# Sixty-four-column pairs for a recurrent attention kernel's large matmuls, and a new split of its DMA queues

## The chip, the cores and the metric

The kernel runs on one core of a Trainium2 chip, in one launch. The metric is the device time of that launch in microseconds, lower is better. TensorE is called PE below, VectorE DVE, ScalarE ACT, GpSimd POOL and SyncE SP.

## What is computed

Four layers are run over one sequence of 2048 tokens of width 512: attention with a recurrent memory (A), a dense layer (B), A again, B again, each with a layer norm in front and a residual around it. A and B use the same weights both times.

```python
def A(x, mem):                         # x: 2048 x 512, mem: 8 x 512
    for s in range(64):                # segments of 32 tokens
        h = concat(mem, x[32*s : 32*s+32])              # 40 x 512
        q, k, v = h @ Wq, h @ Wk, h @ Wv                # 32 heads of 128
        p = softmax(mask(q @ k.T * 128**-0.5))          # per head 40 x 40
        o = concat_heads(p @ v) @ Wo                    # 40 x 512
        mem = o[:8]                                     # goes into the next segment
        out[32*s : 32*s+32] = o[8:]
B = lambda x: relu(x @ w1) @ w2                         # 512 -> 1376 -> 512
x = x + A(layernorm(x), mem0);  x = x + B(layernorm(x))
x = x + A(layernorm(x), mem0);  x = x + B(layernorm(x))
```

The memory ties each segment to the one before it, so the 64 segments of a layer come strictly in turn.

## The kernel before, in words

The two A layers run interleaved: the second starts four segments (`DELTA = 4`) after the first. Step k of 68 handles segment k of the first layer (stream 0) and segment k-4 of the second (stream 1). Steps 0 to 3 have stream 0 alone (40 columns), steps 4 to 63 both (80 columns), steps 64 to 67 stream 1 alone. Weights lie in SBUF throughout.

A step is made of these pieces; the lines are those that the profile shows:

- `step_values`: V for the step's tokens, from the transposed activations `HT`. Steps 4 to 63 use `values` (L973), pairs of matmuls with 64 output columns side by side in the array. Step 0 uses `values_direct` (L1038), steps 1 to 3 use `values_narrow` (L992), four matmuls of 32 columns side by side, whose results reach `V0` by DMA (`place_values`, L1026).
- `queries_keys` (L1074): Q and K of four heads per PSUM bank, 256 matmuls of 128 output columns by 80 a step, evicted to SBUF by ACT or DVE (`copy_on`, L894 and L896).
- `scores` (L1103, 40 columns, pairs side by side), the softmax on DVE and ACT, the transpose of P by a matmul with the identity (`across`, L646), and `attend` (L1187, P times V).
- `project` (L1214): the sum over all heads times `Wo`, 128 matmuls of 128 columns by 80, into one PSUM bank. DVE copies its memory columns into the next step's `HT` (L1230), and this starts the next step's Q and K.
- every second step `finish_pair`: residual, layer norm, dense layer (`across`, L646) for 64 tokens of each layer.

The half of V that doesn't depend on the memory (the first 16 rows of each segment of layer 1) is computed ahead in groups of 128 tokens: groups 0 to 5 (`EARLY = 5`) during start-up (`early_values`, L973), the rest in pairs of groups in later steps (`late_values`, L944, whole 128-column matmuls), spread as work that can fill waits. They go to DRAM (`vh`) and come back by DMA, a segment at a time. Normalized rows go to DRAM too (`xh`) and are read back by `load_group`.

The order of all instructions on all engines is fixed when the program is built, by a list scheduler in the kernel's text (`Plan.order`). It goes by a table of priorities per operation (`PLACE` for PE, `AHEAD` for the others), some constants (`RULE`, `PERIOD`), and costs. Each PE operation has a column mode: `WHOLE` (128 columns), `COL64` (pairs of 64), or `EITHER`, which takes the mode in which the array happens to be; the plan counts `TURN` for each change of mode. `across` writes an `EITHER` operation out: with 64 columns, each 128-column matmul becomes two, on two halves of the array. Before the change the scores and `values` are `COL64`; transposes, `attend` and the first dense matmuls `EITHER`; Q, K, projection and `late_values` `WHOLE`.

DMA queues before: the first quarter of Wv from SP, the other weights from POOL in the order Wv, Wq and Wk by halves, Wo by halves; x rows of the early groups from ACT; early V stores (`vh`) from POOL behind the weights; early `xh` stores from SP, held back until step 1's V is placed. Everything later is on SP.

Of the kernel before, what the change touches and what calls it, by code (L numbers as in the profile page):

```python
# [26 lines left out]
WHOLE, COL64, EITHER, COL32 = range(4)  # L27
TURN = 0.096

RULE = (0.0731, 331.4491, 505.4188, 866559925356557.625)  # L30
PERIOD = 46.2777
PLACE = {
    ("attend.mmu0.0", 0): -152.667, ("attend.mmu0.0", 1): -118.912, ("attend.mmu0.0", 2): -639.225,
    ("attend.mmu0.0", 3): 328.193, ("attend.mmu0.0", 4): -173.499, ("attend.mmu0.0", 5): 386.967,
    ("attend.mmu0.0", 6): 449.133, ("attend.mmu1.0", 0): -183.38, ("attend.mmu1.0", 1): 433.744,
    ("attend.mmu1.0", 2): 361.711, ("attend.mmu1.0", 3): 441.403, ("attend.mmu1.0", 4): -122.568,
    ("attend.mmu1.0", 5): 199.077, ("attend.mmu1.0", 6): 581.404, ("attend.mmu2.0", 0): -862.741,
    ("attend.mmu2.0", 1): -762.821, ("attend.mmu2.0", 2): -99.412, ("attend.mmu2.0", 3): -218.396,
    ("attend.mmu2.0", 4): -720.778, ("attend.mmu2.0", 5): -60.014, ("attend.mmu2.0", 6): -142.579,
    ("attend.mmu3.0", 0): -166.299, ("attend.mmu3.0", 1): -129.893, ("attend.mmu3.0", 2): -1226.967,  # L40
    ("attend.mmu3.0", 3): 67.821, ("attend.mmu3.0", 4): -136.693, ("attend.mmu3.0", 5): -20.817,
    ("attend.mmu3.0", 6): 293.466, ("attend.mmu4.0", 0): 65.898, ("attend.mmu4.0", 1): -215.881,
    ("attend.mmu4.0", 2): 381.601, ("attend.mmu4.0", 3): 412.604, ("attend.mmu4.0", 4): -130.21,
    ("attend.mmu4.0", 5): -853.627, ("attend.mmu4.0", 6): 948.075, ("dense_layer.mm.0", 1): 732.94,
    ("dense_layer.mm.0", 3): 740.199, ("dense_layer.mm.0", 6): 839.326, ("dense_layer.mm.1", 1): -969.556,
    ("dense_layer.mm.1", 3): -286.677, ("dense_layer.mm.1", 6): 67.604, ("dense_layer.mm.2", 1): 398.19,
    ("dense_layer.mm.2", 3): 243.499, ("dense_layer.mm.2", 6): 419.477, ("dense_layer.mm.3", 1): 627.889,
    ("dense_layer.mm.3", 3): 181.496, ("dense_layer.mm.3", 6): 643.035, ("dense_layer.mm.4", 1): 161.37,
    ("dense_layer.mm.4", 3): 390.622, ("dense_layer.mm.4", 6): 400.054, ("dense_layer.mm.5", 1): 594.567,
    ("dense_layer.mm.5", 3): 753.248, ("dense_layer.mm.5", 6): 345.325, ("finish_pair.turn.0", 1): -144.39,  # L50
    ("finish_pair.turn.0", 3): -761.751, ("finish_pair.turn.0", 6): -878.802, ("g0", 2): -907.97,
    ("g1", 2): 259.128, ("g2", 2): -170.342, ("g3", 2): -266.685, ("g4", 2): -99.976, ("g5", 2): 565.774,
    ("late_values.mmv0.0", 0): 283.731, ("late_values.mmv1.0", 0): -248.92, ("late_values.mmv2.0", 0): -1018.714,
    ("late_values.mmv3.0", 0): 469.169, ("late_values.mmv4.0", 0): -1001.105, ("late_values.mmv5.0", 0): 1.489,
    ("late_values.mmv6.0", 0): -868.467, ("late_values.mmv7.0", 0): 433.155, ("layernorm.turn.0", 1): 337.759,
    ("layernorm.turn.0", 3): 441.922, ("layernorm.turn.0", 6): -292.588, ("layernorm.turn.1", 1): -863.663,
    ("layernorm.turn.1", 3): -167.818, ("layernorm.turnr.0", 0): -153.966, ("layernorm.turnr.0", 4): 426.349,
    ("layernorm.turnr.1", 0): 374.651, ("layernorm.turnr.1", 4): 594.017, ("prepare.turns.0", 2): -916.093,
    ("project.mm.0", 0): 352.884, ("project.mm.0", 1): 403.52, ("project.mm.0", 2): 426.265,
    ("project.mm.0", 3): 475.549, ("project.mm.0", 4): -8.363, ("project.mm.0", 5): 481.308,  # L60
    ("project.mm.0", 6): 364.213, ("project.mm.1", 0): 360.97, ("project.mm.1", 1): 250.905,
    ("project.mm.1", 2): 395.025, ("project.mm.1", 3): 90.611, ("project.mm.1", 4): -154.497,
    ("project.mm.1", 5): 342.487, ("project.mm.1", 6): -140.762, ("project.mm.2", 0): 69.475,
    ("project.mm.2", 1): 427.61, ("project.mm.2", 2): -910.526, ("project.mm.2", 3): 539.171,
    ("project.mm.2", 4): -962.774, ("project.mm.2", 5): 327.765, ("project.mm.2", 6): 570.292,
    ("project.mm.3", 0): 234.432, ("project.mm.3", 1): 212.581, ("project.mm.3", 2): 219.168,
    ("project.mm.3", 3): 1057.658, ("project.mm.3", 4): 374.948, ("project.mm.3", 5): 458.206,
    ("project.mm.3", 6): 1049.752, ("project.mm.4", 0): -906.842, ("project.mm.4", 1): -226.675,
    ("project.mm.4", 2): -119.077, ("project.mm.4", 3): 366.414, ("project.mm.4", 4): -955.316,
    ("project.mm.4", 5): 408.222, ("project.mm.4", 6): -222.974, ("queries_keys.mmu0.0", 0): -319.479,  # L70
    ("queries_keys.mmu0.0", 1): -311.142, ("queries_keys.mmu0.0", 2): -195.441,
    ("queries_keys.mmu0.0", 3): -783.942, ("queries_keys.mmu0.0", 4): -856.389,
    ("queries_keys.mmu0.0", 5): -1226.512, ("queries_keys.mmu0.0", 6): -189.749,
    ("queries_keys.mmu0.1", 0): -126.555, ("queries_keys.mmu0.1", 1): -875.245,
    ("queries_keys.mmu0.1", 2): -230.758, ("queries_keys.mmu0.1", 3): -218.806, ("queries_keys.mmu0.1", 4): -924.83,
    ("queries_keys.mmu0.1", 5): -998.214, ("queries_keys.mmu0.1", 6): -798.535, ("queries_keys.mmu0.2", 0): 1.933,
    ("queries_keys.mmu0.2", 1): -915.221, ("queries_keys.mmu0.2", 2): -763.206,
    ("queries_keys.mmu0.2", 3): -815.004, ("queries_keys.mmu0.2", 4): -155.478,
    ("queries_keys.mmu0.2", 5): -920.249, ("queries_keys.mmu0.2", 6): -766.935, ("queries_keys.mmu0.3", 0): -285.59,
    ("queries_keys.mmu0.3", 1): -134.747, ("queries_keys.mmu0.3", 2): 7.492, ("queries_keys.mmu0.3", 3): -23.601,  # L80
    ("queries_keys.mmu0.3", 4): -292.473, ("queries_keys.mmu0.3", 5): -193.042,
    ("queries_keys.mmu0.3", 6): -173.541, ("queries_keys.mmu1.0", 0): -40.306,
    ("queries_keys.mmu1.0", 1): -1010.704, ("queries_keys.mmu1.0", 2): -94.937,
    ("queries_keys.mmu1.0", 3): -233.672, ("queries_keys.mmu1.0", 4): -212.713,
    ("queries_keys.mmu1.0", 5): -961.418, ("queries_keys.mmu1.0", 6): -321.925,
    ("queries_keys.mmu1.1", 0): -965.925, ("queries_keys.mmu1.1", 1): -223.66, ("queries_keys.mmu1.1", 2): -323.504,
    ("queries_keys.mmu1.1", 3): 20.112, ("queries_keys.mmu1.1", 4): -146.653, ("queries_keys.mmu1.1", 5): -223.193,
    ("queries_keys.mmu1.1", 6): -158.937, ("queries_keys.mmu1.2", 0): -823.694,
    ("queries_keys.mmu1.2", 1): -932.252, ("queries_keys.mmu1.2", 2): -231.6, ("queries_keys.mmu1.2", 3): -250.634,
    ("queries_keys.mmu1.2", 4): 237.43, ("queries_keys.mmu1.2", 5): -250.953, ("queries_keys.mmu1.2", 6): -993.941,  # L90
    ("queries_keys.mmu1.3", 0): -189.715, ("queries_keys.mmu1.3", 1): -231.672,
    ("queries_keys.mmu1.3", 2): -257.674, ("queries_keys.mmu1.3", 3): -300.812,
    ("queries_keys.mmu1.3", 4): -145.268, ("queries_keys.mmu1.3", 5): -37.546, ("queries_keys.mmu1.3", 6): -183.014,
    ("queries_keys.mmu2.0", 0): 140.663, ("queries_keys.mmu2.0", 1): -210.356, ("queries_keys.mmu2.0", 2): -294.536,
    ("queries_keys.mmu2.0", 3): -112.732, ("queries_keys.mmu2.0", 4): 320.259, ("queries_keys.mmu2.0", 5): 215.543,
    ("queries_keys.mmu2.0", 6): -122.288, ("queries_keys.mmu2.1", 0): 428.309, ("queries_keys.mmu2.1", 1): 92.511,
    ("queries_keys.mmu2.1", 2): -899.997, ("queries_keys.mmu2.1", 3): 229.222, ("queries_keys.mmu2.1", 4): 280.866,
    ("queries_keys.mmu2.1", 5): 161.233, ("queries_keys.mmu2.1", 6): 27.508, ("queries_keys.mmu2.2", 0): 204.746,
# [82 lines left out]
    ("values_direct.ev", 1): -11.513, ("values_narrow.ev", 1): -7.969,  # L181
}

LOAD = {("v", 0): 4.4, ("v", 1): 3.8, "o": 2.95}
REST, SLOW = 2.75, 6.0

EARLY, SPREAD = 5, (0, 0, 2, 4, 4, 6, 8, 8)


def t_mm(n):  # L190
    return max(0.025, 0.0025 + n / 2400)


# [211 lines left out]
def kernel(  # L405
# [387 lines left out]
    def prepare_group(g, gate=(), first=None):  # L793
# [26 lines left out]
        if g <= EARLY:  # L820
            early_values(g, xnT)
# [530 lines left out]
```

## Time and profile before

| | |
|---|---|
| runs, us | 1633.72, 1636.3, 1640.62 (median 1636.3) |
| the profiled execution | 1633.76 us in all, of which the span of the profile is 1632.0 |
| mean TensorE clock granted | 0.997 of full |
| DVE, ACT, POOL busy | 1111.6, 1052.5, 140.1 us (68%, 64%, 9%) |
| longest rows | L1074 Q and K 355.7 + 349.3 us, L1214 344.5 us, L973 265.9 us |
| DMA moved | 63.89 MB, at 369 and 231 GB/s in the first two fortieths of the span, at most 51 after |
| weights from POOL, median issue to landing | Wq 21.3, Wk 25.8, Wo 36.7 us |

How to read it: the profile shows a matmul from its start to a modelled end, some 0.2 us later, while the next one starts 0.036 us after it. So a "busy" PE hides short waits. The distance between starts is what counts. An engine's own idle time is shown in square brackets with the event that ended it.

### The profile page before, as it was taken

What the parts mean: (1) busy time and instruction counts of PE and PEld (TensorE: products, weight loads), DVE (VectorE), ACT (ScalarE), POOL (GpSimd) and SP (SyncE); (2) the same over time, 40 slices, a digit from 0 to 9 for tenths busy, and PEclk for the clock granted to TensorE, in tenths of its full rate; (3) what the DMA queues carried; (4) which work ended last, traced back from release to release, by engine and by line L of the source; (5) the groups of instructions that cost most, each with busy time, mean ns of one, the idle gap of its engine ahead of it and who ended that gap; (6) DMA issues with size and microseconds to landing.
All of it is one profiled execution on the core that took longest, in us unless ns stands there. A gap on an engine that the chain in (4) does not pass through costs nothing.

```text
span 1632.0 us, 88442 instructions
## 1 busy us (share of the span) xinstructions
PE 1589.6 (97%) x39898; PEld 1377.3 (84%) x39992; DVE 1111.6 (68%) x3091; ACT 1052.5 (64%) x2655; POOL 140.1 (9%) x352
## 2 busy tenths in 40 slices
PE   7999999999999999999999999999999999999997
PEld 4788888888888888888888888888888888888886
DVE  4566776776676676677667667667667767766765
ACT  5566666676666666666667666666666666666664
POOL 3100000000000100000100000100000000000000
PEclk9999999999999999999999999999999999999999
DMA  9720101110110110110110111110110100000000
GB/s 369 231 51 21 27 22 27 41 28 22 28 24 22 41 26 22 25 34 19 38 29 22 28 25 28 35 28 20 28 28 22 26 21 22 19 18 18 18 6 6
DMA packets 47097, 63.89 MB, mean 39 GB/s; under 512 B 17784, under 2 KB 33440, under 8 KB 46720
## 3 DMA queue, kind: packets, MB, share of 16 engines
q1 hardware_dynamic: 41136, 39.09, 10.0%
q0 software_dynamic: 4704, 18.35, 2.9%
q8 instruction: 313, 5.13, 1.4%
q10 hardware_dynamic: 880, 0.80, 0.2%
q14 instruction: 64, 0.52, 0.1%
HBM read 33.50 MB, written 11.93 MB: 28 GB/s over the span
## 4 chain that ended last, share of the span: by engine, by line
PE 92%; DMA 3%; DVE 2%; ACT 2%; issue 1%; POOL 0%; ACTq 0%; SPq 0%; POOLq 0%; DVEq 0%
PE work L1074 37%; PE st L1214 18%; PE fill L973 14%; PE fill L646 10%; PE work L1187 4%; PE work L1103 4%; DMA Wo_sb<-in_A_Wo_dram 2%; PE work L646 2%; PE fill L944 2%; ACT OT L894 1%; DVE HT L1230 0%; PE fill L992 0%; DMA vw<-in_A_x_dram 0%; ACT es L1125 0%; ACT PT L1168 0%
## 5 line engine op out<-in xcount | busy, mean ns | idle before, releaser
L1074 PE MATMUL work<-HT,Wk_sb 128*128 128x80 bf16 (+1 forms) x8704 | 355.7, 199 | 9.6 <-DVE HT L1230 8.8
L1074 PE MATMUL work<-HT,Wq_sb 128*128 128x80 bf16 (+1 forms) x8704 | 349.3, 199 | 1.3 <-DVE HT L1230 0.9
L1214 PE MATMUL st<-OT,Wo_sb 128*128 128x80 bf16 (+1 forms) x8704 | 344.5, 199 | 4.5 <-ACT OT L894 2.5
L1214 PEld LDWEIGHTS <-Wo_sb 128*128 128x128 bf16 x8704 | 324.9, 99 | 28.0 <-issue 5.2
L1074 PEld LDWEIGHTS <-Wq_sb 128*128 128x128 bf16 x8704 | 320.4, 99 | 26.4 <-issue 15.1
L1074 PEld LDWEIGHTS <-Wk_sb 128*128 128x128 bf16 x8704 | 321.6, 99 | 16.4 <-DVE HT L1230 13.3
L894 ACT CAST qT<-work 128x320 bf16<-128x320 f32 (+1 forms) x534 | 219.5, 412 | 76.8 <-PE work L1074 32.4
L973 PE MATMUL fill<-Wv_sb,HT 128*64 128x512 bf16 x2048 | 265.9, 381 | 0.0
L894 ACT CAST kT<-work 128x320 bf16<-128x320 f32 (+1 forms) x510 | 209.9, 412 | 82.5 <-PE work L1074 49.1
L894 ACT CAST OT<-work 128x320 bf16<-128x320 f32 (+1 forms) x404 | 158.1, 417 | 119.8 <-PE work L1187 117.3
L1168 ACT ACTIVATE PT<-work,half 128x320 bf16<-128x320 f32 (+2 forms) x384 | 170.9, 468 | 67.1 <-PE work L646 47.0
L894 ACT CAST vw<-fill 128x512 bf16<-128x512 f32 x203 | 119.0, 586 | 92.5 <-PE fill L973 82.0
L1114 DVE TENSOR_TENSOR es<-work,maskb 128x320 f32<-128x320 f32 (+2 forms) x340 | 136.8, 404 | 45.2 <-PE work L1103 40.3
L1170 DVE TENSOR_SCALAR PT<-work,half 128x160 bf16<-128x160 f32 (+2 forms) x296 | 127.5, 454 | 25.1 <-PE work L646 23.4
L973 PEld LDWEIGHTS <-HT 128*64 128x64 bf16 x2048 | 99.0, 110 | 52.1
L1125 ACT ACTIVATE es<-es 128x320 f32<-128x320 f32 (+2 forms) x340 | 137.6, 410 | 6.0 <-DVE es L1121 5.0
L1121 DVE TENSOR_TENSOR es<-es,mx 128x320 f32<-128x320 f32 (+2 forms) x340 | 136.7, 405 | 5.5
L1118 DVE TENSOR_REDUCE mx<-es 128x8 f32<-128x320 f32 (+2 forms) x340 | 135.2, 400 | 6.2
L1145 DVE TENSOR_TENSOR P<-es,sm 128x320 bf16<-128x320 f32 (+2 forms) x340 | 133.1, 408 | 5.3
L1230 DVE CAST HT<-st 128x64 bf16<-128x64 f32 (+1 forms) x67 | 14.8, 221 | 175.2 <-PE st L1214 175.2
L1128 DVE TENSOR_REDUCE sm<-es 128x8 f32<-128x320 f32 (+2 forms) x340 | 131.6, 396 | 2.5 <-ACT es L1125 1.6
L1103 PEld LDWEIGHTS <-qT 128*40 128x40 bf16 x4096 | 90.8, 98 | 44.8 <-ACT kT L894 10.2
(98 smaller groups left out, 1779.3 us busy)
## 6 DMA issues: line engine op xcount, KB each, us to landing
V<-vw SPq DMA_DIRECT2D x252, 48.0 KB
V<-vh SPq DMA_DIRECT2D x120, 64.0 KB
vh<-vg SPq DMA_DIRECT2D x40, 128.0 KB
Wq_sb<-in_A_Wq_dram POOLq DMA_DIRECT2D x2, 2048.0 KB, 21.3
Wk_sb<-in_A_Wk_dram POOLq DMA_DIRECT2D x2, 2048.0 KB, 25.8
Wo_sb<-in_A_Wo_dram POOLq DMA_DIRECT2D x2, 2048.0 KB, 36.7
Wv_sb<-in_A_Wv_dram POOLq DMA_DIRECT2D x1, 2048.0 KB, 11.8
vh<-w_sb POOLq DMA_DIRECT2D x4, 512.0 KB, 9.9
```

Source lines behind the costliest of these rows:

```text
L646: nc.tensor.matmul(out_[u:v, :], lhsT=lhsT[:, u:v], rhs=rhs, start=start, stop=stop, tile_position=(0, u))
L894: nc.scalar.copy(out=out_, in_=in_)
L973: nc.tensor.matmul(vp[64 * b:64 * b + 64, :], lhsT=cols(c4), rhs=Wv_sb[:, c4, n * 512:(n + 1) * 512], start=(c4 == 0), stop=(c4 == NC4 - 1 ...
L1074: nc.tensor.matmul(qp[:, hi * 2 * L:hi * 2 * L + n], lhsT=W_sb[:, c4, h * Dh:(h + 1) * Dh], rhs=HT[:, c4, c0:c1], start=(c4 == 0), stop=(c ...
L1103: nc.tensor.matmul(v[64 * g2:64 * g2 + L, a, i, b, :], lhsT=qT[:, hi, a * L:(a + 1) * L], rhs=kT[:, hi, a * L:(a + 1) * L], start=True, st ...
L1114: nc.vector.tensor_tensor(out=flat(es[:, A]), in0=flat(sp[:, A]), op=ALU.add, in1=maskb[:, a_lo:a_hi, :].unsqueeze(2).to_broadcast([128, n ...
L1118: nc.vector.tensor_reduce(out=mx[:, As], in_=es3(), axis=AX.X, op=ALU.max)
L1121: nc.vector.tensor_tensor(out=es3(), in0=es3(), op=ALU.subtract, in1=mx[:, As].unsqueeze(2).to_broadcast([128, ns * na, L]))
L1125: nc.scalar.activation(out=es[:, A], in_=es[:, A], func=ACTF.Exp, scale=SCALE)
L1145: (nc.gpsimd if eng == POOL else nc.vector).tensor_tensor(out=o, in0=flat(es[:, A]), op=ALU.mult, in1=sm[:, As].rearrange("p (a s) -> p a ...
L1168: nc.scalar.activation(out=o, in_=i, func=ACTF.Copy, scale=half[:, b:b + 1])
L1214: nc.tensor.matmul(wo[:, 2 * W * c4 + c0:2 * W * c4 + c1], lhsT=Wo_sb[:, h, c4 * 128:(c4 + 1) * 128], rhs=OT[:, h, c0:c1], start=(h == 0 a ...
```

## The change

Q, K and projection get a mode of their own, `SOFT`: where the pair (operation, place in the step pattern) stands in a list (`PAIRED`), the operation is `EITHER`, else `WHOLE`. Such an operation is then written as pairs of 64 columns if the array is in that mode. `late_values` becomes `EITHER` too. The mode `COL32` and `values_narrow` go, and `values_direct`: steps 0 to 3 compute V with `values`, from columns 0 to 63 of `HT`, straight into `V0`, with no DMA, and group 0 has no early V. `EARLY` is 7 instead of 5, so two more groups are computed in start-up, and the late ones are four pairs, each spread over 12 steps instead of 10. The tables of priorities and the constants are new throughout.

All weights, the early `vh` and the early `xh` stores go through SP, in that order; POOL loads the early x rows (before: ACT), and they land in tiles of `hT` (before: of `vw`). The identity no longer waits for the issue of a weight load on POOL.

```diff
-WHOLE, COL64, EITHER, COL32 = range(4)
-TURN = 0.096
+WHOLE, COL64, EITHER, SOFT = range(4)
+TURN, HALVED = 0.096, 1.02
...
+PAIRED = {
+    ("project.mm.0", 1), ("project.mm.0", 2), ("project.mm.0", 4), ("project.mm.1", 0), ("project.mm.1", 1),
...
+}
-EARLY, SPREAD = 5, (0, 0, 2, 4, 4, 6, 8, 8)
+EARLY, SPREAD = 7, (0, 0, 2, 4, 4, 6, 8, 10)
...
+        o.soft = tile == SOFT
+        o.tile = o.mode = tile if not o.soft else EITHER if (o.key, phase(o.step)) in PAIRED else WHOLE
...
-                o.mode = o.tile if o.tile != EITHER else WHOLE if tile == COL32 else tile
+                o.mode = o.tile if o.tile != EITHER else tile
+                if o.soft and o.mode == COL64:
+                    o.end = t + HALVED * o.cost[e]
...
-    def bulk(eng, t, fn, name, size, r=(), w=(), rate=REST):
+    def bulk(t, fn, name, size, r=(), w=(), uses=(), rate=REST, chain=("issue",)):
...
-        plan.op(eng, t, fn, r=r, w=[("issued", *name), *(["issue"] if eng == POOL else [])])
+        plan.op(SP, t, fn, r=[*r, *uses], w=[("issued", *name), *chain])
...
-                q = nc.gpsimd if (c, p0) != ("v", 0) else nc.sync
...
-                    q.dma_start(out=W_s[c][:, :, cs], in_=W_v[c][:, :, cs])
+                    nc.sync.dma_start(out=W_s[c][:, :, cs], in_=W_v[c][:, :, cs])
...
             def load():
-                q.dma_start(out=xb[:, :], in_=A_x[0, 128 * g:128 * (g + 1), :])
+                (nc.gpsimd if early else nc.sync).dma_start(out=xb[:, :], in_=A_x[0, 128 * g:128 * (g + 1), :])
...
-                nc.gpsimd.dma_start(out=vh[g][:, p0:p0 + n, :], in_=room_span(g, p0, n))
+                nc.sync.dma_start(out=vh[g][:, p0:p0 + n, :], in_=room_span(g, p0, n))
...
-        def mm():
+        def mm(cols):
             for c4 in range(NC4):
-                nc.tensor.matmul(vp[:, :], lhsT=xl[:, c4, 0, :, :].rearrange("p g t -> p (g t)"),
-                                 rhs=Wv_sb[:, c4, n * 512:(n + 1) * 512], start=(c4 == 0), stop=(c4 == NC4 - 1))
+                across(cols, vp[:, :], xl[:, c4, 0, :, :].rearrange("p g t -> p (g t)"),
+                       Wv_sb[:, c4, n * 512:(n + 1) * 512], start=(c4 == 0), stop=(c4 == NC4 - 1))
...
-        if k == 0:
-            values_direct(HTs[0][:, :, 0:L], deps)
-            return
-        if 1 in act:
-            values(lambda c4: HTs[i][:, c4, HS:2 * L], lambda p: vw[:, p, :], ("vw",), deps)
+        if k < DELTA:
+            values(lambda c4: HTs[i][:, c4, 0:64], lambda p: V0[:, p, :], lambda p: [("V0", p, b) for b in range(2)], deps)
         else:
-            values_narrow(HTs[i][:, :, HS:HS + 32], deps)
-        place_values(k, False)
+            values(lambda c4: HTs[i][:, c4, HS:2 * L], lambda p: vw[:, p, :], lambda p: [("vw", p)], deps)
+            place_values(k, False)
...
-                        nc.tensor.matmul(qp[:, hi * 2 * L:hi * 2 * L + n], lhsT=W_sb[:, c4, h * Dh:(h + 1) * Dh],
-                                         rhs=HT[:, c4, c0:c1], start=(c4 == 0), stop=(c4 == NC4 - 1))
+                        across(cols, qp[:, hi * 2 * L:hi * 2 * L + n], W_sb[:, c4, h * Dh:(h + 1) * Dh],
+                               HT[:, c4, c0:c1], start=(c4 == 0), stop=(c4 == NC4 - 1))
...
-                        nc.tensor.matmul(wo[:, 2 * W * c4 + c0:2 * W * c4 + c1], lhsT=Wo_sb[:, h, c4 * 128:(c4 + 1) * 128],
-                                         rhs=OT[:, h, c0:c1], start=(h == 0 and c4 == 0), stop=(h == H - 1),
-                                         skip_group_check=True)
+                        across(cols, wo[:, 2 * W * c4 + c0:2 * W * c4 + c1], Wo_sb[:, h, c4 * 128:(c4 + 1) * 128],
+                               OT[:, h, c0:c1], start=(h == 0 and c4 == 0), stop=(h == H - 1), skip_group_check=True)
...
-    start = {g: DELTA + 10 * i for i, g in enumerate(pairs)}
+    start = {g: DELTA + 2 + 12 * i for i, g in enumerate(pairs)}
```

## The prediction

> **What bounds the kernel now.** I read the page's busy times and chain first, then the groups by shape, then PE's timeline of one pair of steps, then the start by windows.
>
> ```profile
> span 1632.0 us, 88442 instructions
> PE 1589.6 (97%) x39898; PEld 1377.3 (84%) x39992; DVE 1111.6 (68%) x3091; ACT 1052.5 (64%) x2655; POOL 140.1 (9%) x352
> PE 92%; DMA 3%; DVE 2%; ACT 2%; issue 1%; POOL 0%; ACTq 0%; SPq 0%; POOLq 0%; DVEq 0%
> ```
>
> PE is busy nearly throughout and holds 92% of the chain that ended last. The other engines have a third of the span free. So I keep an account of PE: work, changes of mode, waits. The groups give the shapes:
>
> ```profile
> L1214 PE MATMUL st<-OT,Wo_sb 128*128 128x80 bf16 x7680 | 313.8, 202 | 2.5 <-ACT OT L894 2.5
> L1187 PE MATMUL work<-PT,V 128*128 128x80 bf16 x644 | 66.4, 202 | 0.8 <-DMA V<-vw 0.4 <-DVE P L1145 0.2
> L1187 PE MATMUL work<-PT,V 128*64 128x80 bf16 x760 | 40.4, 202 | 0.2
> L1214 PEld LDWEIGHTS <-Wo_sb 128*128 128x128 bf16 x8704 | 324.9, 99 | 28.0 <-issue 5.2 <-DMA Wo_sb<-in_A_Wo_dram 1.3
> L1187 PEld LDWEIGHTS <-V 128*64 128x64 bf16 x760 | 33.3, 111 | 4.4 <-issue 0.6
> ```
>
> A mean of 202 ns is latency. The distance between starts is on the timeline (start, duration, engine, line, names, shape, count), here the end of a step without spare work:
>
> ```profile
> 1397.85 0.20 PE L1187 MATMUL work<-PT,vw 128*64 128x80 bf16 x2
> 1397.99 0.75 PE L1074 MATMUL work<-HT,Wq_sb 128*128 128x80 bf16 x16
> 1398.57 0.74 PE L1074 MATMUL work<-HT,Wk_sb 128*128 128x80 bf16 x16
> ...
> 1399.40 0.20 PE L1187 MATMUL work<-PT,vw 128*128 128x80 bf16 x1
> 1399.83 0.32 PE L646 MATMUL work<-ident,P 128*128 128x80 bf16 x4 [0.23 <-ACT es L1125]
> 1400.17 0.27 PE L1103 MATMUL work<-kT,qT 128*40 128x40 bf16 x8
> 1400.38 1.32 PE L1214 MATMUL st<-OT,Wo_sb 128*128 128x80 bf16 x32
> ...
> 1403.18 0.24 PE L646 MATMUL work<-ident,P 128*128 128x80 bf16 x2
> 1403.57 1.31 PE L1214 MATMUL st<-OT,Wo_sb 128*128 128x80 bf16 x32 [0.15 <-ACT OT L894]
> ...
> 1404.86 1.41 PE L1214 MATMUL st<-OT,Wo_sb 128*128 128x80 bf16 x32
> 1406.59 0.75 PE L1074 MATMUL work<-HT,Wk_sb 128*128 128x80 bf16 x16 [0.32 <-DVE HT L1230]
> ```
>
> 16 matmuls from 1397.99 to 1398.57 are 0.036 us each. The two halves at 1397.85 take until 1397.99: 0.036 and 0.10 more, a change of mode. Over steps 8 to 63 the trace's starts give 0.096 us for 128 to 64 columns, 0.098 back; I use 0.097. The waits here: 0.39 before P at 1399.83, 0.10 beside the mode change before 1400.17, 0.32 before 1403.57, and from 1404.86, 32 matmuls (1.15) leave 0.58 of 1.73, of which 0.11 lies inside L1214 and 0.49 is the wait for HT. About 1.4 in sum.
>
> The trace's weight loads are complete (39,992, as in the program), so each instruction in the program's order has a time. Work is priced by distances of undisturbed runs: 0.036 (80 columns), 0.216 (512), 0.056 (128), 0.025 (40), half for each of a 64-column pair (0.0175 measured in L1187), 0.013 for the scores. In us:
>
> ```
> steps      time    work   changes  waits
> 0          45.5    36.5     14      7.7
> 1-3        54.3    42.8     32      8.4
> 4-7        95.4    89.9     24      3.2
> 8-63     1346.5  1289.5    280     29.8
> 64-end     78.4    68.3     25      7.7
> all      1620.1  1527.0    375     56.7
> ```
>
> PE starts at 7.4 us; the rest lies around it. In the waits of 8-63, an even step has 0.07; an odd one 1.50 without spare work (six of them), 1.01 with one late-values operation, 0.70 or 0.18 with two. The start is set by weights:
>
> ```profile
> 50.83 1.78 PE L1214 MATMUL st<-OT,Wo_sb 128*128 128x40 bf16 x64 [1.19 <-DMA Wo_sb<-in_A_Wo_dram]
> 50.00:52.00 2.00, 1.17 (x46) 1.17 (x47) 0.00 (x0) 0.00 (x0) 0.00 (x0) 1.00 1.03 414
> 54.00:56.00 2.00, 2.00 (x25) 0.80 (x25) 0.00 (x0) 0.29 (x1) 0.00 (x0) 0.50 0.65 258
> ```
>
> PE waits for the last half of Wo with the DMA engines full (share 1.03), and two windows later its clock is halved (0.50).
>
> **What the Trainium skill says.** TensorEngine Tiling (Array Packing), Tiling Modes: changing the tiling mode drains TensorE; agreed, at 0.097 us. The same page, Restrictions: column tiling disables fast weight load. The trace agrees that a 64-column load takes longer (111 against 99 ns), but the halves still start 0.0175 apart. TensorE: Matmul & The Clock Gate, Part 1: after an idle window of about 3.4 us the clock falls to half; the trace shows one such window, from 52.9 to 56.4 us. DMA: Bandwidth & Descriptors, Issuing engines are not separate DMA queues: all queues share the 16 engines, another issuer saves only issue time; the start above fits, as the engines are full whatever the queue.
>
> **The change, part by part.** The changed program's instruction order is known without running it, and I count in it.
>
> *Changes of mode.* 375 become 285: step 0 14 to 1, steps 1-3 32 to 15, 4-7 24 to 20, 8-63 280 to 224 (odd steps 6 to 4), end 25 and 25. 90 x 0.097 = -8.7.
>
> *Pairs.* Of 80-column work 2,944 projections and 976 Q/K matmuls become pairs, 40-column ones 896. Twice as many instructions, 6,544 more matmuls in all. Price per pair: nothing, from L1187. Bounds: L1187's runs give 35 ns a pair against 36 (-4 us); above, the 12 ns by which a 64-column load is longer would be +116 us if it showed twice a pair, which L1187 excludes, so one nanosecond, the grain of the starts: +5. I take 0.
>
> *Work.* Steps 1-3 compute V with 4 operations instead of 2: 6 x 0.86 = +5.2. Group 0's early V goes: 4 x 0.86 = -3.5. Sum +1.7 (1528.7). Two more groups move from steps 8-63 to the start, so that the start has 176.5 of work (before 169.1), the middle 1283.9 (1289.5).
>
> *Start.* All weights must pass before the last Wo half, whichever queue carries them. Between 4 and 6 us, with the first quarter of Wv on SP's queue alone, 393 to 408 GB/s flowed, later from POOL's 385 to 414. So I leave step 0's end at 52.4 (Wo at 50.8, then 1.6 of pairs): wait 45.0-38.7-0.1 = 6.2 against 7.7. The early stores stand behind Wo on SP, as they did on POOL; the read-back of group 1 and w1/w2 stand behind them, but PE wants w1 only after step 2 and the read-back at step 4. V stores of groups 6 and 7 stand before w2's loads; if PE is late with those groups, w2 is late too, but some 20 us lie between. POOL drops 8 weight and 6 store issues (0.55 to 1.28 us each on its timeline) and takes seven x loads among its norm operations; a group's rows late by 1 us would move filling work only, inside the 6.2. Steps 1-3: V0 no longer waits for DMA, two groups of V (6.9) fill, the halved clock (1.7 lost) has less cause: 4.5 instead of 8.4. Steps 4-7: 2.5 instead of 3.2. Together -6.0; bounds 0 (nothing filled) and -10.
>
> *Waits, steps 8-63.* In odd steps without spare work (six), P stands 3.90 of work behind its scores instead of 3.69, and the scores before L1214 0.69 behind their K: about 0.33 of the 0.49 stays. The 0.32 stays. The 0.11 inside L1214 goes under the change of mode that now stands there. The HT wait stays. So 1.24 for 1.50: -1.6. The other 22: one late operation always stands before P, so that 0.9 is left; in 7 a second stands on the boundary and covers HT (0.4), in 3 a transpose covers part (0.56). Sum 12 x 0.9 + 7 x 0.4 + 3 x 0.56 = 15.3 against 16.1. Together -2.4. Bounds: -8 (all odd waits as in the best steps) and +10, if the new order opens waits of 0.2 us a step that counting can't show.
>
> Sum: -8.7 + 0 + 1.7 - 6.0 - 2.4 = -15.4. The profiled execution took 1633.8, so 1618.4. The median of the runs stands 2.5 above it; scaled, 1620.9, rounded to 1620.
>
> **The rivals.** 0.5%, 8 us, is about what a measurement here can tell from no change. Times are against the median.
> *The saved time turns into waits.* Odd steps already wait on evictions; if the shorter PE stretches only lengthen those, the 5.4 saved in 8-63 and the 2.4 are lost, and the start gives half: -8.7+5.4+1.7-3.0 = -4.6, 1632. For it: 1.5 us of waits in steps without spare work. Against: the changes removed lie where 22 of 28 odd steps have spare work ahead. 0.14.
> *Slower: long runs of halves don't hold 0.0175.* Place: the projection of odd steps, some 250 halves in a row, where the longest 80-column run in the trace is 47. Price: 4,816 pairs times the excess; it decides at 15.4/4816 = 3.2 ns a pair. At 6 ns (17%) +29, less 15.4: about 1650. For it: longer weight loads, twice the instructions. Against: the scores' halves come 0.013 apart. 0.11.
> *The start gives more*: waits as in steps 4-7 and no halved clock, -20 in all: 1616. For it: the full list of work behind Wo; against: one stream's chain of softmax and projection. 0.15.
>
> **Chances and range.** Forecast 0.60, more 0.15, absorbed 0.14, slower 0.11. Faster by over 0.5% is 0.75, within 0.14, slower 0.11. The range: 1608 (start -10, middle -8, pairs -4, with the other terms -29) to 1632 (absorbed case); the slower case and the tail of the others, 0.2, lie outside.
>
> **What would show it.** Changes of mode about 225 in 8-63 and their 0.097; halves in L1214 0.0175 to 0.018 apart; an odd step without spare work 22.2 instead of 22.6; first Wo use of the second half near 50.8; no half clock in the start. Wrong if halves come over 0.021 apart, Wo lands after 53, or odd steps wait over 1.5.

## The result and the profile after

| | before | after |
|---|---|---|
| runs, us (median) | 1633.72 to 1640.62 (1637.39), 4 runs | 1688.19 to 1695.94 (1692.01), 4 runs |
| ratio | | 1.0334, 95% interval 1.0301 to 1.0367 |
| profiled execution, us | 1633.76 | 1695.94, span 1694.2 |

The changed kernel is 3.3% slower, where the forecast was 1% faster. `across`, which now writes Q, K, projection and transposes, stands at L674, `attend` at L1166, the scores at L1082. First the busy times and the chain of waits from the page of after, and the row of its third part for the queue that carries instructions (packets, MB, share of 16 engines' span):

```profile
span 1694.2 us, 101526 instructions
PE 1608.3 (95%) x46536; PEld 1392.0 (82%) x46536; DVE 1077.6 (64%) x3040; ACT 1082.6 (64%) x2703; POOL 127.2 (8%) x346
...
q8 instruction: 364, 5.96, 1.5%
...
PE 85%; issue 3%; DVE 3%; ACT 1%; DVEq 0%; POOLq 0%; POOL 0%; ACTq 0%
```

PE is still the busiest engine by far, but its share of the chain fell from 92 to 85%, and "issue", time in which PE waits for nothing that the profile shows, rose from 1 to 3%. The groups by shape say where:

```profile
L674 PE MATMUL st<-OT,Wo_sb 128*128 128x80 bf16 x4736 | 195.9, 202 | 5.8 <-issue 5.8
...
L674 PE MATMUL st<-OT,Wo_sb 128*64 128x80 bf16 x5888 | 127.6, 202 | 30.0 <-issue 28.0 <-ACT OT L926 1.0
...
L674 PEld LDWEIGHTS <-Wo_sb 128*64 128x64 bf16 x6400 | 128.2, 113 | 42.9 <-issue 39.2
```

The halves of the projection had 30.0 us of idle time ahead of them, 28.0 of it ended by no engine, DMA or semaphore. Before, the largest such wait of L1214 had been for ACT. PE's waits over the whole run, summed by what ended them (us, times, longest us), repeat this:

```profile
PE st L674 <- issue: 39.4, 42, 2.8
PE fill L674 <- DVE xr L725: 10.8, 2, 7.5
PE work L674 <- issue: 9.7, 10, 2.6
PE work L674 <- DVE HT L1208: 6.6, 21, 0.3
PE work L1166 <- issue: 5.9, 6, 1.1
```

On PE's timeline of one odd step (start, duration, engine, line, names, shape, count, idle time before) one sees such waits one by one:

```profile
766.96 0.70 PE L674 MATMUL st<-OT,Wo_sb 128*64 128x80 bf16 x29
768.11 0.81 PE L674 MATMUL st<-OT,Wo_sb 128*64 128x80 bf16 x35 [0.45 <-issue]
...
769.17 0.24 PE L674 MATMUL work<-ident,P 128*64 128x80 bf16 x4
769.24 0.29 PE L674 MATMUL fill<-ident,xr 128*64 128x64 bf16 x8
769.57 1.20 PE L674 MATMUL st<-OT,Wo_sb 128*64 128x80 bf16 x57
772.04 0.33 PE L674 MATMUL st<-OT,Wo_sb 128*64 128x80 bf16 x7 [1.27 <-issue]
```

Two things are to be seen. While they run, the halves keep their pace: 57 matmuls of 80 columns in 1.20 us, less the latency of 0.2, are 0.018 us each. And the breaks split one operation in the middle, 29 and 35, 57 and 7, where no program order asks for a wait. From the first break to the second PE ran exactly 128 matmuls: 35, then 24 of `attend` in the lines left out, 4, 8 and 57.

The count 128 points to the instruction stream. A matmul and its weight load are two instructions, so 128 matmuls are 256. PE's 93,072 instructions (46,536 and 46,536) by 256 are 363.6, and the instruction queue moved 364 packets, 5.96 MB by 364 being 16.4 KB each. Before, twice the 39,992 weight loads by 256 are 312.4, with 313 packets. So each packet holds 256 of PE's instructions. A count over the whole trace agrees: if PE's 188 other instructions (waits for semaphores, mostly) are counted too, all 53 waits on "issue" above 0.3 us stand at the same place, within one, in a count by 256. In the records of that queue most packets take 0.9 to 1.4 us, and where PE stops in steps 8 to 63, packets start mostly 3.4 to 4.4 us apart. 256 instructions of whole 128-column matmuls last 128 x 0.036 = 4.6 us, of halves 128 x 0.018 = 2.3.

In the start the single breaks are longest. PE's timeline there:

```profile
31.66 0.46 PE L674 MATMUL work<-HT,Wk_sb 128*64 128x40 bf16 x17 [2.16 <-issue]
...
37.45 0.69 PE L674 MATMUL work<-HT,Wq_sb 128*64 128x40 bf16 x32
...
44.60 2.70 PE L674 MATMUL work<-HT,Wk_sb 128*64 128x40 bf16 x93 [2.64 <-issue]
...
57.00 2.15 PE L674 MATMUL st<-OT,Wo_sb 128*64 128x40 bf16 x97 [2.79 <-issue]
...
67.74 0.71 PE L674 MATMUL st<-OT,Wo_sb 128*64 128x40 bf16 x33 [1.19 <-issue]
```

and windows over the middle of it (busy time of PE, PEld, DVE, ACT, POOL, each with its count, then granted clock, DMA share, GB/s):

```profile
40.00:50.00 10.00, 7.36 (x178) 5.69 (x176) 3.61 (x14) 3.12 (x8) 0.79 (x2) 0.72 1.09 355
50.00:60.00 10.00, 7.21 (x250) 5.99 (x248) 4.87 (x21) 2.79 (x9) 0.84 (x2) 0.84 1.03 377
```

Here the moving data have 40 columns, and the instruction packets share full DMA engines with the weights (share 1.03 to 1.09). The breaks grow to 2.8 us, and the clock falls below full after them: four stretches at half clock before 140 us, 20.5 us in all, where the kernel before had one of 3.4. The page TensorE: Matmul & The Clock Gate of the Trainium skill, Part 1, ties the half clock to an idle window of about 3.4 us. This trace agrees that idle time goes ahead of it, but not on the length: no break here is longer than 2.8 us, and ahead of the half clock at 75.0 us they were 0.8 and 1.2 us; before, the wait shown ahead of it was 1.19. The measurement decides.

The row at 37.45 shows a second thing. 32 halves of 40 columns at full clock take 0.69 us, less a latency of 0.18, so they come 0.016 us apart. The prediction priced them at half of a whole one, 0.0125. At 40 columns a pair costs 0.032 us against 0.025 for a whole matmul.

The account of PE by phase, made as in the prediction (time / work / changes of mode / waits), for after:

```
steps      time    work   changes  waits   (waits before)
0          60.7    38.7      1      22.0      7.7
1-3        64.5    47.5     15      15.5      8.4
4-7        97.9    90.3     20       5.6      3.2
8-63     1380.6  1283.9    224      75.0     29.8
64-end     79.0    68.3     25       8.2      7.7
all      1682.6  1528.7    285     126.3     56.7
```

The counts of matmuls and of changes of mode are those forecast. Work here is that count at the prediction's prices, so anything that ran slower than its price, at half clock or in 40-column halves, stands under the waits, and so the whole loss does. Odd steps of 8-63 wait 1.6 to 4.0 us each, even ones next to nothing (one, step 26, about 0.4).

### The profile page after: what moved, and what is told of

Same layout as the page of the kernel before. It is cut to its first block, busy times and chain, and to the rows that moved or that the text cites. A ratio compares the mean times of both kernels' runs of the same rounds, so it can differ in the third digit from the quotient of the medians.

```text
span 1694.2 us, 101526 instructions
## 1 busy us (share of the span) xinstructions
PE 1608.3 (95%) x46536; PEld 1392.0 (82%) x46536; DVE 1077.6 (64%) x3040; ACT 1082.6 (64%) x2703; POOL 127.2 (8%) x346
## 3 DMA queue, kind: packets, MB, share of 16 engines
q8 instruction: 364, 5.96, 1.5%
## 4 chain that ended last, share of the span: by engine, by line
PE 85%; issue 3%; DVE 3%; ACT 1%; DVEq 0%; POOLq 0%; POOL 0%; ACTq 0%
PE work L674 35%; PE st L674 18%; PE fill L999 12%; PE fill L674 12%; PE work L1166 4%; PE work L1082 3%; DVE es L1093 1%; DVE mx L1097 0%; DVE sm L1107 0%; DVE es L1100 0%; DVE HT L1208 0%; DVE P L1124 0%; PE fill L797 0%; ACT OT L926 0%; DVE PT L1149 0%
## 5 line engine op out<-in xcount | busy, mean ns | idle before, releaser
L674 PE MATMUL st<-OT,Wo_sb 128*64 128x80 bf16 (+3 forms) x11904 | 356.5, 200 | 41.6 <-issue 39.4
L674 PEld LDWEIGHTS <-Wo_sb 128*64 128x64 bf16 (+1 forms) x11904 | 329.9, 107 | 61.1 <-issue 46.9
L674 PE MATMUL work<-HT,Wk_sb 128*128 128x80 bf16 (+3 forms) x9536 | 358.5, 200 | 6.6 <-issue 6.3
L674 PEld LDWEIGHTS <-Wq_sb 128*128 128x128 bf16 (+1 forms) x9488 | 328.4, 102 | 41.3 <-issue 15.2
L674 PE MATMUL work<-HT,Wq_sb 128*128 128x80 bf16 (+3 forms) x9488 | 352.2, 200 | 8.3 <-DVE HT L1208 6.4
L674 PEld LDWEIGHTS <-Wk_sb 128*128 128x128 bf16 (+1 forms) x9536 | 327.0, 103 | 9.2 <-issue 6.7
L1147 ACT ACTIVATE PT<-work,half 128x320 bf16<-128x320 f32 (+2 forms) x438 | 193.4, 467 | 49.6 <-PE work L674 32.6
L926 ACT CAST OT<-work 128x320 bf16<-128x320 f32 (+1 forms) x366 | 144.7, 417 | 91.4 <-PE work L1166 91.4
L1149 DVE TENSOR_SCALAR PT<-work,half 128x320 bf16<-128x320 f32 (+2 forms) x242 | 106.9, 452 | 28.7 <-PE work L674 16.6
L928 DVE CAST OT<-work 128x320 bf16<-128x320 f32 (+1 forms) x178 | 76.6, 450 | 59.7 <-PE work L1166 59.7
```

The source lines that it names most:

```text
L674: nc.tensor.matmul(out_[u:v, :], lhsT=lhsT[:, u:v], rhs=rhs, start=start, stop=stop, tile_position=(0, u), **more)
L926: nc.scalar.copy(out=out_, in_=in_)
L928: nc.vector.tensor_copy(out=out_, in_=in_)
L1147: nc.scalar.activation(out=o, in_=i, func=ACTF.Copy, scale=half[:, b:b + 1])
L1149: nc.vector.tensor_scalar_mul(out=o, in0=i, scalar1=half[:, b:b + 1])
```

## The experiments

The theory under test, S, is that PE outruns its instruction supply where many halves follow each other. Its rivals are named in the expectations.

**All of the new order, no pairs.** The changed kernel's order of operations on every engine is kept as it is, and only the way an operation is written out is changed: a `SOFT` operation is always whole, and the others, the late values among them, go by their own mode as before. There are 383 changes of mode. Since the array is then less often in the mode of 64 columns, operations that go either way are written whole more often too: besides the 4,816 pairs of Q, K and projection, 1,308 pairs of `attend`, transposes and the like go (46,536 matmuls become 40,412). The four further kernels with a condition, below, put another one in the place of `False`.

```diff
+        at = WHOLE
         for o in plan.order():
...
-            elif o.soft or o.tile == EITHER:
-                o.fn(64 if o.mode == COL64 else 128)
+            pair = o.tile == EITHER and (not o.soft or False)
+            at = at if pair else WHOLE if o.soft else at if o.tile == EITHER else o.tile
+            if o.soft or o.tile == EITHER:
+                o.fn(64 if at == COL64 else 128)
```

> The changed kernel in its own order, with Q, K and projection always written as whole 128-column matmuls; operations that may go either way take the mode the array is in. Changes of mode 383 instead of 285 (+9.5 us). Theory S (supply): PE runs out of instructions when halves follow each other for long; in the changed kernel 48 stalls in steps 8-63 (about 50 us) and 11 in steps 0-3 (16 us) stand exactly 128 weight loads or a multiple apart, and they cost some half-clock windows too (7 us). Then all of these go: about 1692 - 50 - 16 - 7 + 9.5 = 1628 (1620 to 1638). Theory O (order): the new order itself brings waits; then the time stays at 1690 to 1702. Theory Q (the single SyncE queue makes the start late): the start, steps 0-3, stays 25 us longer than before, the rest recovers: about 1650.

Measured: 1630.2 us (1628.9 to 1630.39), ratio to before 0.9959 (0.9945 to 0.9973). That is S: the new order and the new queues, which this version keeps, are not the cause of the loss; the same order without pairs is faster than the changed kernel by 61.8 us and than the kernel before by 0.4%. The windows of this run over the stretch shown above:

```profile
40.00:50.00 10.00, 8.27 (x195) 6.05 (x193) 6.61 (x29) 3.87 (x12) 0.86 (x2) 1.00 1.09 356
50.00:60.00 10.00, 9.57 (x240) 6.97 (x236) 3.00 (x10) 5.13 (x13) 0.61 (x1) 1.00 1.05 392
```

The DMA engines are as full as in after, and PE is busy longer at full clock. A small rest of the same wait is left even here, where 40-column whole matmuls come 0.025 us apart:

```profile
45.42 1.40 PE L674 MATMUL st<-OT,Wo_sb 128*128 128x40 bf16 x49
48.55 0.55 PE L674 MATMUL st<-OT,Wo_sb 128*128 128x40 bf16 x15 [1.73 <-issue]
```

**Pairs only in the start, and only later.** Conditions `o.step < DELTA` (351 changes) and `o.step >= DELTA` (317).

> As e1, but pairs allowed in steps 0 to 3; changes of mode 351. Theory S: the start stays as in the changed kernel (16 us of stalls, half-clock windows), the middle recovers: 1692 - 50 + 6.4 = about 1648. Theory O: 1690 to 1700. Theory Q: as e1, within 10 us of it.

> As e1, but pairs allowed from step 4 on; changes of mode 317. Theory S: the start recovers, the middle keeps its 50 us of stalls: 1692 - 16 - 7 + 3.1 = about 1672. Theory Q: no gain from this edit, about 1695.

Measured: 1650.08 us (1647.88 to 1650.6), ratio 1.0083 (1.0068 to 1.0099), and 1670.57 (1668.76 to 1673.12), ratio 1.0212 (1.0197 to 1.0228). S had 1648 and 1672. Over the version without pairs they lose 19.9 and 40.4 us, 60.3 in sum, and the changed kernel loses 1692.0 - 1630.2 = 61.8. The two parts account for the whole.

By the distances between starts in the traces of the changed kernel and of the version without pairs, PE waits 126.3 against 50.9 us. Of this difference of 75.4, breaks on "issue" make some 63, matmuls at half clock some 8, and the slower pace of 40-column halves at full clock some 5. From step 4 on it is almost breaks alone; in steps 0 to 3 breaks make only about 11. Pairs in the start alone bring 17 us at half clock before 140 us, late pairs alone 3.4, as without pairs.

**PE alone.** A kernel that does nothing but rows of matmuls of one shape, executed once, to see whether the array or the supply is slow (C is the rival that halves are slow in the array).

> PE alone, nothing of the reference computed: long runs of one kind of matmul, each with its own weight load: 1024 of 128 columns by 80, 2048 halves by 80, 2048 of 128 columns by 40, 2048 halves by 40, 1024 halves by 80 beside 8 MB of loads, 128 halves by 512. Theory S: whatever the column mode, PE gets about 128 load-and-matmul pairs per 4.0 to 4.3 us, so 0.031 to 0.034 us each: 128x80 at 0.036 without stalls, the three fast kinds all at about 0.032 with a stall after each 128, longer beside the loads. Theory C (halves are slow in the array, from slower weight loads): 128x40 at 0.025 without stalls, halves by 80 evenly above 0.018.

PE's timeline, first whole, then halves, whole ones with 40 columns of moving data, halves with 40, and at last halves by 80 while 8 MB are loaded:

```profile
37.52 36.85 PE L31 MATMUL bank<-xs,W 128*128 128x80 bf16 x1024 [1.11 <-DVE xs L36]
...
80.67 2.48 PE L31 MATMUL bank<-xs,W 128*64 128x80 bf16 x128 [1.00 <-issue]
84.40 2.48 PE L31 MATMUL bank<-xs,W 128*64 128x80 bf16 x128 [1.24 <-issue]
88.12 2.48 PE L31 MATMUL bank<-xs,W 128*64 128x80 bf16 x128 [1.24 <-issue]
...
147.50 3.35 PE L31 MATMUL bank<-xs,W 128*128 128x40 bf16 x128 [0.38 <-issue]
151.51 3.35 PE L31 MATMUL bank<-xs,W 128*128 128x40 bf16 x128 [0.65 <-issue]
...
192.10 2.18 PE L31 MATMUL bank<-xs,W 128*64 128x40 bf16 x127 [0.50 <-DVE xs L36]
...
261.86 2.48 PE L31 MATMUL bank<-xs,W 128*64 128x80 bf16 x128 [2.95 <-issue]
267.79 4.48 PE L31 MATMUL bank<-xs,W 128*64 128x80 bf16 x128 [3.44 <-issue]
```

1024 whole matmuls run through. Of halves by 80, after a first row of 255, 128 run, at 2.28 / 127 = 0.018 us each, then PE stops, again and again, so that 128 cost 3.45 to 4.0 us, 27 to 31 ns a matmul. Whole matmuls of 40 columns, which no tiling touches, stop too, though less often. So the stops come neither from the array nor from the tiling but from the number of instructions in a time, and for halves by 80 C falls. All 36 waits on "issue" above 0.3 us in this kernel, too, stand at one place in a count by 256. Beside the loads 128 cost 5.9 us.

For halves by 40 C holds in part: 2.00 / 126 = 0.016 us each at full clock, where half of 0.025 was assumed. Their later rows ran mostly at half clock and say nothing about the supply. Every matmul here, as in the kernels, has its own weight load; what a row without them would do is open.

**Which late pairs cost.** Late pairs are of two kinds, Q and K (992 pairs, up to 96 halves in a row) and projection (2,944 pairs, up to 248 in a row). Conditions `(o.step >= DELTA and o.kind.startswith('queries_keys'))` and `(... 'project')`.

> The changed kernel's order; only Q and K of steps 4 on may run as pairs (992 pairs, some 32 matmuls in a row), projection and the start stay whole: 319 changes of mode where the version with everything whole has 383. S (instruction supply: a pair costs nothing until a stretch of halves has used up what was fetched ahead, and 64 halves in a row do not): the changes saved, 64 x 0.097 = 6.2 us, below the 1630 of the whole version: 1624, with hardly a wait of PE on nothing. R (each pair of late steps costs the same wherever it stands: 46.6 us over 3,936 pairs in the version with late pairs alone, 11.8 ns each): 992 x 0.0118 - 6.2 = +5.5: 1636.

> The changed kernel's order; only the projections of steps 4 on may run as pairs (2,944 pairs, up to 256 halves in a row), Q and K and the start stay whole: 381 changes of mode against 383. S: nearly all of the late loss is here, 35 to 46 us, for two changes of mode saved: 1665 to 1676, in some 30 to 40 waits on nothing of about 1 us, 128 matmuls apart, in the odd steps' projection. R (11.8 ns a pair): 2,944 x 0.0118 = 34.7, 1665, the distances all a little longer.

Measured: Q and K alone 1625.26 us (1624.21 to 1626.36), ratio 0.9937 (0.9922 to 0.9952); projection alone 1659.78 (1656.37 to 1660.51), ratio 1.0145 (1.0127 to 1.0162). The first number is S's, and a fixed price per pair falls: 992 pairs cost next to nothing and bring 4.9 us below the version without pairs, nearly the 6.2 of the 64 changes of mode saved. The second was expected at least 5 us higher by both theories and doesn't tell them apart. What is certain there is the kind of loss, from the waits of the run with projection pairs:

```profile
PE st L674 <- issue: 21.4, 34, 1.7
PE fill L674 <- DVE xr L725: 10.8, 2, 7.5
PE work L674 <- DVE HT L1208: 6.6, 21, 0.3
PE work L1166 <- issue: 2.7, 5, 0.7
```

and that the kinds don't add: 29.6 for projection, -4.9 for Q and K, but 40.4 for both. In odd steps the Q and K pairs stand ahead of the projection, so together they may use up more of what was fetched ahead; no run tests this by itself.

**The plan made anew.** The list `PAIRED` is cut, to nothing or to two entries, `("queries_keys.mmu4.0", 1)` and `("queries_keys.mmu4.1", 1)`, and the scheduler orders the work with it.

> The changed kernel with an empty list of pairs, planned anew: 367 changes of mode against the whole version's 383 in the old plan's order. S and R alike: 16 x 0.097 = 1.6 us below the whole version's 1630.2, so 1628.6, if the plan opens no waits. It is the yardstick for the version with two entries in the list.

> The changed kernel with the list of pairs cut to two entries, Q and K of the last four heads in odd steps, and the plan made anew with it: 307 changes of mode. S: work 1528.7 as in the whole version, 76 changes fewer (-7.4 us), waits as there if the new plan opens none: 1623, range 1620 to 1628. R: 992 pairs of 11.8 ns take it back: 1634.

Measured: 1705.19 us (ratio 1.0436, 1.041 to 1.0461) and 1638.95 (1.002, 1.0012 to 1.0027). Both expectations missed, since "if the plan opens no waits" did not hold. PE's waits with the empty list:

```profile
PE st L654 <- ACT OT L906: 23.1, 57, 0.5
PE work L1146 <- ACT PT L1127: 22.3, 30, 0.8
PE work L654 <- DVE HT L1188: 11.4, 35, 0.7
```

These are ordinary waits for evictions, 45 us on ACT alone; waits on supply sum to 1.5 us. The clock adds to them: 55 us at half clock against 13 in the version without pairs, though no wait in the rows shown is longer than 0.8. The tables of priorities fit one list of pairs and not another, so taking the list out and planning anew measures the order, not the pairs. Only the kernels that keep the order do that. Part of the two-entry version's distance is of this kind too (its steps 1-3 wait 11.0 us, against 1.9 with the same pairs in the old order); the rest of it wasn't followed up.

**The queues.** In the version with Q and K pairs the weights but the first quarter of Wv, and the early V stores, go back to POOL, everything else unchanged.

```diff
+                q = nc.gpsimd if (c, p0) != ("v", 0) else nc.sync
...
-                    nc.sync.dma_start(out=W_s[c][:, :, cs], in_=W_v[c][:, :, cs])
+                    q.dma_start(out=W_s[c][:, :, cs], in_=W_v[c][:, :, cs])
...
-                nc.sync.dma_start(out=vh[g][:, p0:p0 + n, :], in_=room_span(g, p0, n))
+                nc.gpsimd.dma_start(out=vh[g][:, p0:p0 + n, :], in_=room_span(g, p0, n))
```

> The version with only the late pairs of Q and K (1625.3 us), with one part of the change undone: all weights but the first quarter of Wv, and the early V stores, are issued by POOL again, in the same order of work on PE. Q (the prediction's term: the bytes ahead of the last half of Wo set its arrival, whichever queue carries them): the same within 2 us, 1623 to 1627. U (the queue is worth something by itself: 14 issues of 0.55 to 1.28 us each stand among POOL's norm operations and x loads again, so groups come late and PE waits more in the first 60 us): 3 to 9 us slower, 1628 to 1634.

Measured: 1641.97 us (1640.08 to 1644.18), ratio 1.0045 (1.0032 to 1.0059), 16.7 slower than with SP and more than either side expected. PE's longest waits there, then the seven row loads there (KB each, median us from issue to landing), and third the same loads in the version with weights on SP:

```profile
PE fill L675 <- DVE xr L726: 20.1, 4, 7.7
...
PE fill L1000 <- DVE xg L929: 4.3, 1, 4.3
```

```profile
hT<-in_A_x_dram POOLq DMA_DIRECT2D x7, 128.0 KB, 11.7
```

```profile
hT<-in_A_x_dram POOLq DMA_DIRECT2D x7, 128.0 KB, 5.4
```

The rows of x now stand in one queue with the weights, and behind them. That is not the split of the kernel before, where ACT loaded the rows. One more edit tells queue from issuing engine: `(nc.scalar if early else nc.sync)` in the place of `(nc.gpsimd if early else nc.sync)` for the early rows.

> The version with weights and early V stores on POOL (1642.0 us), with the seven early x-row loads issued by ACT instead of POOL, so that rows and weights are again in queues of different engines, split as in the kernel before. F (rows behind weights in one queue: the rows took 11.7 us from issue to landing there, 5.4 where the weights were in SP's queue): the start recovers, 1624 to 1630, rows landing in 5 to 7 us. I (issuing weights costs POOL time that its norm operations need): it stays near 1640, or loses more, since seven issues of some 0.6 us are added to ACT.

Measured: 1625.75 us (1623.54 to 1625.97), ratio 0.9936 (0.9922 to 0.9949). Weights on POOL with rows on ACT take as long as weights on SP with rows on POOL (1625.26); rows and weights together on POOL cost 16 us. POOL's own time was not short there: after the fifth row load, issued at 29.09 us, and one store it stood idle for 15 us, until 45.25. For the rows on ACT the profile gives no landing time, so the 5 to 7 us of F stay unseen.

## Why the prediction was wrong

The step that failed is the pairs: "Price per pair: nothing, from L1187", with its upper bound: "one nanosecond, the grain of the starts: +5". The same order with and without pairs (the first experiment's trace) gives the price: waits of 126.3 against 50.9 us, so 75.4, of which the 98 changes of mode that pairs save give back 9.5. Put on the 4,816 pairs of the forecast that is 15.7 ns a pair in the mean; on all 6,124 that differ, 12.3. Forecast was zero. What the runs showed in its place is not a price per pair but breaks of the instruction supply, some 63 of the 75.4 us, where many short matmuls follow each other; half clock and the pace of 40-column halves, in the start, make the rest. By its terms, in us against before:

| term | forecast | after | order without pairs | with late Q and K pairs |
|---|---|---|---|---|
| changes of mode | -8.7 | -8.7 | +0.8 | -5.4 |
| work | +1.7 | +1.7 | +1.7 | +1.7 |
| waits, steps 0-7 | -6.0 | +23.8 | -3.5 | -3.1 |
| waits, steps 8-63 | -2.4 | +45.2 | -3.4 | -2.8 |
| waits, end | 0 | +0.5 | +1.1 | +1.3 |
| sum | -15.4 | +62.5 | -3.3 | -8.3 |

*Pairs.* L1187 told the truth about the array at 80 columns: as long as instructions are there, a half takes 0.018 us, in after as in the measurement by itself. It says nothing of 40 columns, where 896 of the pairs are and a half takes 0.016 instead of 0.0125. And it could not tell of the supply, because only short rows of halves by 80 follow each other in the kernel before (the prediction gives 47; in its trace's weight loads no unbroken row is longer than 24), and by itself PE ran 255 of them before the first break. The prediction noted "twice the instructions" and the 6,544 more matmuls, and gave them no price. The rival "long runs of halves don't hold 0.0175" had the place (odd steps' projection) and the sign, at 0.11, and the mechanism only as a hint; its reason against, scores 0.013 apart, fails in the same way as L1187, since the scores come 8 or 16 at a time. It also looked only at the projection. Of the prediction's signs of being wrong, "odd steps wait over 1.5" came true (1.6 to 4.0) and "halves come over 0.021 apart" did not, since the halves keep their pace between breaks. A third of the loss, 19.9 us, is in the start, where the pairs had been charged nothing.

*Changes of mode.* Right in number and price. But counting by kind would have shown what they cost: of the 98 that the pairs save, 32 are in the start (383 against 351), 64 come with late Q and K (383 against 319), and 2 with the 2,944 pairs of the projection (383 against 381), which lose 29.6 us.

*Start.* -6.0 was near: without pairs -3.5, of which the three waits on supply that stand there take away 1.7 + 0.4 + 1.9. The term "whichever queue carries them" holds for the weights as far as the time of the whole kernel shows it, 1625.75 against 1625.26 us in the last experiment. What it leaves out is that rows must not share that queue. The prediction cited the page DMA: Bandwidth & Descriptors of the Trainium skill, Issuing engines are not separate DMA queues, for issue time being all that another issuer saves; here the 11.7 against 5.4 us and the 16 us of the whole kernel say that it also decides what a transfer stands behind, and the measurement decides. "No half clock in the start" came true with late Q and K pairs, in the version without pairs up to 67.9 us, and not in after.

*Waits of steps 8-63.* -2.4, measured -3.4 and -2.8 where there are no breaks. The sum was near, but in part by luck: in the order with late Q and K pairs (the trace with weights on POOL has all its records) the six steps without spare work wait 1.5 to 1.6 us each, where 1.24 was counted, and the others somewhat less than counted.

*Range.* 1608 to 1632 held the version without pairs and the one with late Q and K pairs. The mistake was to bound an unseen load by rows with short runs.

## What to carry to other kernels

Before splitting small matmuls in two, count PE instructions per time: in these runs 256 of them took 3.4 to 4.4 us to arrive, and about 6 beside full DMA engines, so a long row of weight loads and matmuls that take less than some 0.03 us each can stop. Rows of up to 96 halves by 80 cost next to nothing here, rows of up to 248 cost 29.6 us; where the limit lies between them was not measured. Split where a run is short and a change of mode is saved, and leave long runs whole. Measure the pace of a half at the width at which it will be used. Judge a planner's option by rewriting it in a fixed order, because a new plan measures its own tables.

The best version measured is the changed kernel with only the late Q and K pairs kept, 1625.26 us, 0.9937 of before.

## What the runs showed of the hardware

- PE's instructions come in packets of 16.4 KB, 256 instructions each (364 packets for 93,072). A stretch of 128 loads and matmuls at 2.3 us took 3.45 to 4.0 us with idle DMA engines and 5.9 beside an 8 MB load; the break stands in the profile as "issue", 0.97 to 1.52 us and up to 3.44.
- Two halves with 80 columns take 0.036 us, as a whole matmul does; two with 40 columns take 0.032, where a whole one takes 0.025.
- Where there were more breaks, there was more half clock: 20.5 us in the start of after, 17 with pairs in the start alone, 3.4 without pairs and before.
- Rows of 128 KB landed 5.4 us after their issue in a queue of their own and 11.7 behind weights in one queue, at the same total of bytes.
